# Attention and two expert layers on one core: the first group's next scores issued between a slot's two products, and two tiles one slot later

## The chip, the core and the metric

The kernel runs on one core of a Trainium2 chip. A core has four compute engines, each with an in-order queue of its own: TensorE (PE, with its weight loads as PEld), VectorE (DVE), ScalarE (ACT) and GpSimd (POOL). SyncE (SP) issues most of the DMA transfers. An engine waits for another through semaphores, and what stands behind a waiting instruction in the same queue waits too. The metric is the time of one execution on the device in microseconds (us).

## The reference, cut to what matters

Three stages follow one another: attention over keys and values pooled by 8, a layer with the gate `h * cos(h)`, and a layer of 8 experts of which each token uses one.

```python
# attention: batch 8, heads 8, seq 576, head_dim 64
k_p = k.reshape(B, H, Sp, 8, D).mean(axis=3); v_p = ...   # 72 pooled keys
scores = scale * q @ k_p.T
scores = scores - max(scores);  attn = exp(scores);  attn /= sum(attn) + 1e-9
x = attn @ v_p                       # to 4608 tokens x 512
h = x @ w_in                         # 512 -> 2048
x2 = (h * cos(h)) @ w_out            # 2048 -> 512
expert = argmax(x2 @ w_gate)         # 8 experts
out = gate * relu(x2 @ w1[expert]) @ w2[expert]
```

## The kernel before

The 4608 tokens are worked through in 12 groups of 384 (`g`), each of three tiles of 128 tokens. A group has 16 slots (`s`), one for each 128 columns of the hidden layer. In every slot the order is written out by hand, and each engine's queue keeps it:

- `mm1(s)`, on PE: the first product of the slot, 12 matmuls into one of two banks `HB[s % 2]`. It needs that bank back from `chain_b(s - 2)`.
- `mm2(s - 2)`, on PE: the second product, 9 matmuls on `gh` and `gl` of two slots earlier.
- `chain_a(s)`: ACT scales (L382) and rounds (L383), DVE subtracts (L385), ACT takes the sine (L386).
- `chain_b(s)`: DVE multiplies and frees the bank (L391), ACT rounds to `gh` (L392), POOL makes the rest `gl` (L393). In group 0 the `chain_b(s - 1)` is issued inside slot `s`.
- `ex[s]`: a list of further work, issued at the slot's end.

In group 0 alone the weights are also decoded, by `weights()`, which `chain_a` calls between L383 and L385: `w_bits(s + 3)` puts six DVE operations (two each of L497, L498 and L499) through the two PSUM banks 6 and 7 and has `chain_b(s - 1)` after the second of them; `w_parts(s + 2)` has two ACT casts and two POOL subtractions (L504, L505), `w_scale(s + 4)` two ACT operations (L492), and `w_load(s + 5)` two DMA loads. There are 16 pairs, so `w_bits` ends with slot 12 and `w_parts` with slot 13.

The attention of group 1 is prepared in group 0 by `ex`. For a tile `i`, `scores` has 16 PE matmuls (32 for the tile that lies across two batches) into banks 6 and 7, then on DVE a maximum and a subtraction for each bank (L322, L324), then an exponential on ACT (L330). `norm` has a sum on DVE (L335), which needs the exponential, two small DVE operations and a POOL multiplication (L338). `transp` has eight PE transposes through the same two banks (L345) and a copy on ACT (L349) and on DVE (L351). Tile 1 is kept where the decoded pair 14 has been, and tile 2 where pair 15 has been, so their subtractions wait until POOL has read these pairs. At the end of slot 14 DVE has four sums of the values (`pool_v`, L304) as well; `transp(2)` is issued in slot 15 between the two products, and `pv` (L362 on PE), the attention products of group 1, right behind the 16 slots.

The sine and the exponential are in different function tables of ACT; a table load stands in ACT's queue where the function changes.

Of the kernel before, what the change touches and what calls it, by code (L numbers as in the profile page):

```python
# [14 lines left out]
AF = mybir.ActivationFunctionType  # L15
# [14 lines left out]
NCH = DFF // 128  # L30
# [46 lines left out]
def attention_moe_kernel(ctx, tc, qT, kT, vP, w_in, w_out, wg, w1, w2, cst, tri, wgt, out, dbg=None):  # L77
    nc = tc.nc
    PE, ACT, DVE, POOL, SP = nc.tensor, nc.scalar, nc.vector, nc.gpsimd, nc.sync
# [175 lines left out]
    atts = [pxp.tile([128, H * KP], F32, name="att")] + [w_tmp(6 + i)[:, 0:576] for i in range(2)]  # L255
    atts = [x.rearrange("p (h k) -> p h k", h=H) for x in atts]
# [46 lines left out]
        t = vraw.pop((b, c))  # L303
        DVE.tensor_reduce(vp[b % 2][:, 128 * c:128 * c + 128], t.rearrange("p (f j) -> p f j", j=8), axis=AX.X, op=ALU.add)  # L304

    def scores(T, i, act=False):
        t0 = i * TP
        att, mx, rs = atts[i % len(atts)], mxs[:, i], rss[:, i]
        b0, b1 = T * TP // S, (T * TP + TP - 1) // S
        sc = [rot(), rot()]  # L310
        for pr in range(4):
            for h, r in enumerate((slice(0, 64), slice(64, 128))):
                o = sc[h][:, KP * pr:KP * pr + KP]
                if b0 == b1:
                    PE.matmul(o, lhsT=qs[r, pr, t0:t0 + TP], rhs=kp[b0 % 2][r, pr], start=True, stop=True)
                else:
                    PE.matmul(o[0:64], lhsT=qs[r, pr, t0:t0 + 64], rhs=kp[b0 % 2][r, pr], start=True, stop=True)
                    PE.matmul(o[64:128], lhsT=qs[r, pr, t0 + 64:t0 + TP], rhs=kp[b1 % 2][r, pr], start=True, stop=True)
        vs = [x[:, 0:288].rearrange("p (h k) -> p h k", h=4) for x in sc]
        for hf in range(2):  # L320
            m = mx[:, hf::2]
            DVE.tensor_reduce(m, vs[hf], axis=AX.X, op=ALU.max)  # L322
            if not act:
                DVE.tensor_tensor(att[:, hf::2], vs[hf], m.unsqueeze(2).to_broadcast([128, 4, KP]), op=ALU.subtract)  # L324
        if act:
            DVE.tensor_scalar(mx, mx, -1.0 / 64.0, None, op0=ALU.mult)
            for h in range(H):
                ACT.activation(att[:, h], vs[h % 2][:, h // 2], AF.Exp, scale=1.0 / 64.0, bias=mx[:, h:h + 1], accum_out=rs[:, h:h + 1])
        else:
            ACT.activation(att, att, AF.Exp, scale=1.0 / 64.0)  # L330

    def norm(i, act=False):
        att, rs = atts[i % len(atts)], rss[:, i]
# [34 lines left out]
    def mm1(s):  # L368
        o = HB[s % 2][:, 0:GT]
        n = 0  # L370
        for c in range(4):
            wh, wl = WI[:, 0, c, s * 128:s * 128 + 128], WI[:, 1, c, s * 128:s * 128 + 128]
            for a, x in ((wh, xTh), (wh, xTl), (wl, xTh)):
                PE.matmul(o, lhsT=a, rhs=x[:, c], start=n == 0, stop=n == 11)  # L374
                n += 1
# [198 lines left out]
    norm(0, True)  # L574
    pool_v(0, 1)
    scores(2, 2)
    norm(1, True)
    norm(2)
# [38 lines left out]
        return [E1[0][:, 1024 * k:1024 * k + 1024].rearrange("p (c t) -> p c t", c=4)[:, :, 128 * i:128 * i + 128] for k in range(2)]  # L617

    for g in range(NG):
        ex = {s: [] for s in range(NCH)}  # L620

        def at(s, f, *a):
            ex[s].append(lambda: f(*a))

        if g + 1 < NG:
            for i in range(3):
                if g == 0:
                    at((9, 12, 13)[i], scores, 3 * (g + 1) + i, i)
                    at((9, 12, 13)[i], norm, i)
                    if i < 2:  # L630
                        at((11, 14)[i], transp, i)
                else:
                    at(1 + 4 * i, scores, 3 * (g + 1) + i, i)
                    if i == 0 and g > 1:
                        at(1, route_exp, g - 2)
                    at(1 + 4 * i, norm, i)
                    at(4 + 4 * i, transp, i)
            if g + 2 < NG:
                at(10 if g > 0 else 14, load_q, g + 2)
        dots = {}  # L640
        if g > 0:
            last = g == NG - 1
            n = 0
            for s, k in enumerate((0, 4, 4, 4, 4, 4, 4) if last else (0, 1, 3, 3, 2, 1, 3, 2, 2, 1, 2, 4)):
                dots[s] = list(range(n, n + k))
                n += k
            if last:
                at(1, route_exp, g - 2)
                at(7, route_sel, g - 1)
                at(8, route_exp, g - 1)  # L650
                at(9, route_pos)
                for i in range(3):
                    at(10 + i // 2, route_put, i)
            else:
                at(12, route_sel, g - 1)
                at(14, route_pos)
        if g > 1:
            for i in range(3):
                at(2 + i // 2, route_put, i)
        for b in range(1, B):  # L660
            if g == max(0, b * S // GT - 2):
                if b == 1:
                    at(11, lambda: (kvb.__setitem__(slice(0, None), ring[2:4] + ring[0:2]), kvb_i.__setitem__(0, -1)))
                for c in range(4):
                    if b == 1:
                        at(c // 2, pool_k, b, c)
                        at(11 + c // 2, load_v, b, c)
                        at(14, pool_v, b, c)
                    else:
                        at(2 + 2 * c, pool_k, b, c)  # L670
                        at(2 * c, load_k, b, c)
                if b > 1:
                    for c in range(4):
                        at((7, 10, 12, 14)[c], pool_v, b, c)
                        at((5, 7, 10, 12)[c], load_v, b, c)
        for s in range(NCH):
            mm1(s)
            first_x = s == NCH - 1 and g == NG - 1
            if first_x:
                for i in range(2):  # L680
                    tx_pe(i, XP[i])
            if s == 0 and g > 0:
                mm2(15)
            if s == NCH - 1 and g == 0:
                transp(2)
            elif s == NCH - 1 and g + 1 < NG:
                for c in range(2):
                    pv(g + 1, c)
            if s >= 2:
                mm2(s - 2)  # L690

            def weights():
                w_bits(s + 3, {2: lambda: chain_b(s - 1)} if s > 0 else {})
                w_parts(s + 2)
                w_scale(s + 4)
                w_load(s + 5)

            if g == 0:
                chain_a(s, weights)
            elif g == NG - 1 and 6 < s < 15:  # L700
                c = (s - 7,)
                chain_a(s, lambda: split(0, -50, 0, c, False, (0,)))
            else:
                chain_a(s)
            if s == 0 and g > 0:
                evac(g - 1)
            if first_x:
                E1.append(ep.tile([128, 4096], F32R, name="E1", tag="e1"))
                for i in range(2):
                    tx_parts(XP[i], *unit_x(i))  # L710
            todo = dots.get(s, [])
            if todo:
                route_dot(g - 1, todo.pop(0))
            if g > 0 or s == NCH - 1:
                chain_b(s)
            for n in todo:
                route_dot(g - 1, n)
            if s == NCH - 1 and 0 < g < NG - 1:
                pv(g + 1, 2)
                pv(g + 1, 3)  # L720
            for f in ex[s]:
                f()
            if g == NG - 1:
                if s == 0:
                    SP.dma_start(out=EF[:, 0:4096], in_=w1[0])
                    SP.dma_start(out=wgs, in_=wg)
                    blank()
                if s == 7:
                    SP.dma_start(out=wgb, in_=w2[0])
                if s == 9:  # L730
                    DVE.tensor_scalar(run[:, 0:1], run[:, 0:1], float(EARLY * TP), None, op0=ALU.max)
                if s == 11:
                    SP.dma_start(out=first, in_=tbl[0:EARLY * TP].rearrange("(t p) two -> p t two", p=TP))
                if s == 13:
                    POOL.tensor_copy(firsti, first[:, :, 0])
                    gather(0, 0)
                    gather(0, 1)
                if 6 < s < 15:
                    split(0, -50, 0, c, False, (1,))
        if g == 0:  # L740
            SP.dma_start(out=wgb, in_=wgt.unsqueeze(0).to_broadcast([128, NE * DM]))
            kvb[:] = ldt
            del atts[1:]
            pv(1, 0)
            pv(1, 1)
            mm2(14)
            pv(1, 2)
            pv(1, 3)
        elif g < NG - 1:
            mm2(14)  # L750
# [174 lines left out]
    V, W, L, T = {}, {}, {}, {}  # L925
# [106 lines left out]
```

## Time and profile before

| | |
|---|---|
| median of 3 runs | 1498.08 us (1495.77 to 1500.23) |
| the profiled execution, its own time | 1489.18 us |
| its span, first to last instruction | 1487.4 us |
| mean granted TensorE clock | 0.988 |
| busy share of the span: PE, DVE, ACT, POOL | 96%, 61%, 52%, 32% |

The profiled execution is 8.90 us shorter than the median of the runs; between its time and its span lie 1.78 us. A matmul's end is modelled, so busy shares of PE say less than the gaps between its instructions. In a timeline row the bracket gives the idle time of the engine right before the row and what ended it; a row that merges several instructions of one form has its count at the end. The times in a row are pipelined: an instruction's duration can reach a little into the next one's.

### The profile page before, as it was taken

What the parts mean: (1) busy time and instruction counts of PE and PEld (TensorE: products, weight loads), DVE (VectorE), ACT (ScalarE), POOL (GpSimd) and SP (SyncE); (2) the same over time, 40 slices, a digit from 0 to 9 for tenths busy, and PEclk for the clock granted to TensorE, in tenths of its full rate; (3) what the DMA queues carried; (4) which work ended last, traced back from release to release, by engine and by line L of the source; (5) the groups of instructions that cost most, each with busy time, mean ns of one, the idle gap of its engine ahead of it and who ended that gap; (6) DMA issues with size and microseconds to landing.
All of it is one profiled execution on the core that took longest, in us unless ns stands there. A gap on an engine that the chain in (4) does not pass through costs nothing. (4 is left out here: it accounts for less than half of the span.)

```text
span 1487.4 us, 24388 instructions
## 1 busy us (share of the span) xinstructions
PE 1426.9 (96%) x8394; PEld 1250.2 (84%) x8394; DVE 913.4 (61%) x1997; ACT 777.6 (52%) x1431; POOL 480.5 (32%) x450
## 2 busy tenths in 40 slices
PE   5889999999999999999999999999999999899996
PEld 3768888888888888888888888789999998789996
DVE  7987868675868675868776667552432524772221
ACT  5986656565656565657566655731411413661111
POOL 2662323242424232424232334422221413442121
PEclk9999999999999999999999999999999999999998
DMA  9542112000211100212100002218331402511110
GB/s 299 192 154 108 62 38 69 30 23 30 62 45 43 53 5 22 70 38 62 46 22 22 22 1 80 72 38 342 110 142 38 171 29 82 199 38 60 32 50 23
DMA packets 44119, 112.48 MB, mean 76 GB/s; under 512 B 8025, under 2 KB 24033, under 8 KB 41712
## 3 DMA queue, kind: packets, MB, share of 16 engines
q1 hardware_dynamic: 33184, 78.20, 16.2%
q0 software_dynamic: 9840, 18.98, 4.1%
q10 hardware_dynamic: 864, 12.58, 2.2%
q8 instruction: 100, 1.64, 0.5%
q14 instruction: 131, 1.07, 0.3%
HBM read 98.95 MB, written 20.25 MB: 80 GB/s over the span
## 5 line engine op out<-in xcount | busy, mean ns | idle before, releaser
L374 PE MATMUL bank<-xh,WI 128*128 128x384 f32 x1536 | 435.3, 344 | 10.1 <-DVE tA L391 5.9
L400 PE MATMUL bank<-wb,gh 128*128 128x512 f32 x1152 | 395.1, 397 | 0.0
L374 PEld LDWEIGHTS bank<-xh,WI 128*128 128x128 f32 x1536 | 282.2, 189 | 27.7 <-DVE tA L391 12.6
L400 PEld LDWEIGHTS bank<-wb,gh 128*128 128x128 f32 x1152 | 216.6, 188 | 53.4 <-issue 5.3
L374 PE MATMUL bank<-xl,WI 128*128 128x384 f32 x768 | 259.5, 338 | 1.0 <-DVE xl L366 1.0
L400 PE MATMUL bank<-wb,gl 128*128 128x512 f32 x576 | 227.9, 396 | 0.2 <-POOL gl L393 0.2
L432 DVE SCALAR_TENSOR_TENSOR E<-x2t,wgb 128x512 bf16<-128x512 f32 x264 | 217.9, 825 | 2.1
L782 PEld LDWEIGHTS bank<-E,wb 128*128 128x128 f32 x1632 | 210.4, 192 | 8.9 <-DVEq L809 0.6
L782 PE MATMUL bank<-E,wb 128*128 128x256 f32 x1632 | 213.7, 284 | 0.2 <-DVEq L809 0.2
L792 PE MATMUL bank<-wb,xh 128*128 128x512 f32 x816 | 209.5, 395 | 0.0
L785 ACT ACTIVATE xh<-bank 128x256 fp32r<-128x256 f32 x136 | 52.2, 384 | 279.2 <-PE bank L782 273.2
L786 DVE SCALAR_TENSOR_TENSOR xh<-bank,xh 128x256 fp32r<-128x256 f32 x136 | 57.6, 423 | 218.3 <-ACT xh L785 103.8
L393 POOL TENSOR_TENSOR gl<-E,gh 128x384 fp32r<-128x384 f32 x96 | 104.8, 1092 | 268.2 <-ACT gh L392 234.8
L393 POOL TENSOR_TENSOR gl<-tA,gh 128x384 fp32r<-128x384 f32 x96 | 107.2, 1116 | 247.3 <-ACT gh L392 241.3
L792 PEld LDWEIGHTS bank<-wb,xh 128*128 128x128 f32 x816 | 145.7, 189 | 25.2 <-issue 0.2
L374 PEld LDWEIGHTS bank<-xl,WI 128*128 128x128 f32 x768 | 145.2, 189 | 5.9 <-DVE xl L366 1.9
L195 POOL DMA_INDIRECT E<-x2d,E x66 | 71.2, 1079 | 239.0 <-PE bank L609 213.2
L400 PEld LDWEIGHTS bank<-wb,gl 128*128 128x128 f32 x576 | 108.3, 188 | 18.1 <-POOL gl L393 0.5
L385 DVE SCALAR_TENSOR_TENSOR tA<-bank,tA 128x384 f32<-128x384 f32 x96 | 52.2, 544 | 76.1 <-ACT bank L383 75.7
L385 DVE SCALAR_TENSOR_TENSOR E<-bank,E 128x384 f32<-128x384 f32 x96 | 53.2, 554 | 68.5 <-ACT bank L383 68.5
L234 DVE TENSOR_TENSOR wb<-stg,wb 128x512 fp32r<-128x512 f32 x95 | 70.2, 779 | 23.3 <-ACT wb L232 21.6
L386 ACT ACTIVATE E<-E 128x384 f32<-128x384 f32 x96 | 50.4, 525 | 63.3 <-DVE E L385 62.8
(195 smaller groups left out, 1870.8 us busy)
## 6 DMA issues: line engine op xcount, KB each, us to landing
stg<-w SPq DMA_DIRECT2D x8, 2048.0 KB
stg<-w ACTq DMA_DIRECT2D x6, 2048.0 KB
x2d<-x2t SPq DMA_DIRECT2D x36, 256.0 KB
early<-qT SPq DMA_DIRECT2D x11, 768.0 KB
E<-kT SPq DMA_DIRECT2D x24, 288.0 KB
E<-vP SPq DMA_DIRECT2D x24, 288.0 KB
wgb<-w_in SPq DMA_DIRECT2D x13, 512.0 KB
wgb<-w_out SPq DMA_DIRECT2D x13, 512.0 KB
```

Of the source, the lines that this page charges most:

```text
L195: POOL.indirect_dma_start(out=xg[i], out_offset=None, in_=x2d[0:n], in_offset=bass.IndirectOffsetOnAxis(ap=column(u, i)[0], axis=0), bound ...
L234: ins.append((POOL if pool and c in (2, 5) else DVE).tensor_tensor(l, s, h.bitcast(F32), op=ALU.subtract))
L374: PE.matmul(o, lhsT=a, rhs=x[:, c], start=n == 0, stop=n == 11)
L385: DVE.scalar_tensor_tensor(a, r, MAGIC, a, op0=ALU.subtract, op1=ALU.subtract)
L386: ACT.activation(a, a, AF.Sin, scale=-TWOPI)
L393: POOL.tensor_tensor(gl[s % 2], a, gh[s % 2].bitcast(F32), op=ALU.subtract)
L400: PE.matmul(ACC[i], lhsT=a[:, sl], rhs=w_tile(s)[:, DM * w:DM * w + DM], start=s == 0 and n == 0, stop=s == NCH - 1 and n == 2)
L432: DVE.scalar_tensor_tensor(junk, x2[i], 1.0, wgb[:, DM * e:DM * e + DM], op0=ALU.mult, op1=ALU.mult, accum_out=lgs[:, i, e:e + 1])
L782: PE.matmul(o, lhsT=w_tile(4 * w + s // 2)[:, f], rhs=x[:, c], start=n == 0, stop=n == 11)
L785: ACT.activation(h, o, AF.Relu)
L786: DVE.scalar_tensor_tensor(l, o, 0.0, h.bitcast(F32), op0=ALU.max, op1=ALU.subtract)
L792: PE.matmul(OP[i], lhsT=a[s % 3][:, 128 * i:128 * i + 128], rhs=w_piece(w, s), start=s == 0 and n == 0, stop=s == 7 and n == 2)
```

## The change

`scores` no longer issues the exponential in group 0; that goes to a function of its own, `scores_exp`. The matmuls, maxima and subtractions of `scores` are issued from a table `mid`, right after `mm1(s)` and so ahead of `mm2(s - 2)`, `chain_a(s)` and the decoding in it. The exponential and `norm` stay in `ex[s]`, at the slot's end. Tile 0 stays in slot 9; tile 1 goes from slot 12 to 13, tile 2 from 13 to 14. `transp(0)` stays in slot 11, `transp(1)` in slot 14 (now ahead of the exponential of tile 2), `transp(2)` in slot 15. Groups 1 to 10 are as they were.

```diff
-    def scores(T, i, act=False):
+    def scores(T, i, act=False, then=True):
...
-        else:
-            ACT.activation(att, att, AF.Exp, scale=1.0 / 64.0)
+        elif then:
+            scores_exp(i)
+
+    def scores_exp(i):
+        att = atts[i % len(atts)]
+        ACT.activation(att, att, AF.Exp, scale=1.0 / 64.0)
...
-        ex = {s: [] for s in range(NCH)}
+        ex, mid = {s: [] for s in range(NCH)}, {}
...
                 if g == 0:
-                    at((9, 12, 13)[i], scores, 3 * (g + 1) + i, i)
-                    at((9, 12, 13)[i], norm, i)
+                    mid[(9, 13, 14)[i]] = lambda i=i: scores(3 + i, i, then=False)
+                    at((9, 13, 14)[i], scores_exp, i)
+                    at((9, 13, 14)[i], norm, i)
                     if i < 2:
                         at((11, 14)[i], transp, i)
...
             mm1(s)
+            mid.get(s, bool)()
```

## Rows read from the trace of the kernel before

**Rows 1.** Busy time of each engine, instructions, granted clock, by stretch.
```profile
121.00:200.00 79.00, 78.77 (x451) 68.27 (x450) 59.75 (x136) 49.47 (x85) 22.48 (x20) 1.00 0.22 77
```

**Rows 2.** Waits of PE from 78.8 to 127 us: total, times, longest.
```profile
PE bank L315 <- DVE x2t L499: 2.0, 2, 1.8
...
PE bank L317 <- DVE x2t L499: 0.6, 2, 0.5
```

**Rows 3.** Timeline of DVE, slots 9 to 15 of group 0: start, us, what.
```profile
78.79 1.27 DVE L497 TENSOR_SCALAR bank<-wgb 128x512 uint32<-128x512 uint32 x2
...
82.83 0.55 DVE L385 SCALAR_TENSOR_TENSOR E<-bank,E 128x384 f32<-128x384 f32 x1
83.91 0.46 DVE L322 TENSOR_REDUCE mxs<-bank 128x4 f32<-128x288 f32 x1 [0.53 <-PE bank L315]
...
86.46 0.75 DVE L335 TENSOR_REDUCE rss<-att 128x8 f32<-128x576 f32 x1 [0.75 <-ACT att L330]
...
87.58 1.26 DVE L497 TENSOR_SCALAR bank<-wgb 128x512 uint32<-128x512 uint32 x2
...
102.56 0.55 DVE L385 SCALAR_TENSOR_TENSOR tA<-bank,tA 128x384 f32<-128x384 f32 x1
103.37 0.46 DVE L322 TENSOR_REDUCE mxs<-bank 128x4 f32<-128x288 f32 x1 [0.26 <-PE bank L318]
...
104.99 0.46 DVE L324 TENSOR_TENSOR E<-bank,mxs 128x288 f32<-128x288 f32 x1 [0.24 <-POOL wb L505]
106.20 0.75 DVE L335 TENSOR_REDUCE rss<-E 128x8 f32<-128x576 f32 x1 [0.75 <-ACT E L330]
...
108.86 0.46 DVE L322 TENSOR_REDUCE mxs<-bank 128x4 f32<-128x288 f32 x1 [0.57 <-PE bank L315]
110.96 0.46 DVE L324 TENSOR_TENSOR x2t<-bank,mxs 128x288 f32<-128x288 f32 x1 [1.65 <-POOL wb L505]
...
112.22 0.46 DVE L324 TENSOR_TENSOR x2t<-bank,mxs 128x288 f32<-128x288 f32 x1 [0.44 <-POOL wb L505]
113.43 0.75 DVE L335 TENSOR_REDUCE rss<-x2t 128x8 f32<-128x576 f32 x1 [0.75 <-ACT x2t L330]
...
120.53 0.68 DVE L351 COPY early<-bank 72x512 f32<-72x512 f32 x1
```

**Rows 4.** Timeline of PE, slots 9 to 15 of group 0.
```profile
78.30 0.39 PE L400 MATMUL bank<-wb,gh 128*128 128x512 f32 x1
...
97.29 0.42 PE L374 MATMUL bank<-xh,WI 128*128 128x384 f32 x1
...
107.71 1.11 PE L315 MATMUL bank<-E,early 64*128 64x72 f32 x16
...
121.12 1.57 PE L362 MATMUL bank<-early,E 72*64 72x192 f32 x16
```

**Rows 5.** Timeline of ACT, slots 9 to 14 of group 0.
```profile
83.96 1.28 ACT L330 ACT_TABLE_LOAD   x1
85.75 0.69 ACT L330 ACTIVATE att<-att 128x576 f32<-128x576 f32 x1 [0.51 <-DVE att L324]
...
92.05 1.28 ACT L386 ACT_TABLE_LOAD   x1
93.34 0.52 ACT L386 ACTIVATE tA<-tA 128x384 f32<-128x384 f32 x1
...
107.86 0.51 ACT L392 CAST gh<-tA 128x384 fp32r<-128x384 f32 x1 [0.60 <-DVE tA L391]
108.28 1.14 ACT L504 CAST wb<-x2t 128x512 fp32r<-128x512 f32 x2
```

**Rows 6.** Timeline of PE: the longest wait between two products of group 0.
```profile
43.21 0.69 PE L374 MATMUL bank<-xh,WI 128*128 128x384 f32 x1 [4.51 <-DVE tA L391]
```

**Rows 7.** Busy time by stretch around that wait; the granted clock is third from last.
```profile
40.00:45.00 5.00, 1.79 (x6) 1.79 (x7) 5.00 (x10) 4.77 (x9) 2.19 (x3) 0.60 0.60 212
45.00:50.00 5.00, 5.00 (x20) 4.54 (x19) 5.00 (x9) 3.60 (x8) 2.76 (x3) 0.72 0.62 210
```

## The prediction

> **What bounds the kernel now.** I read the windows first, to see where a lost microsecond can be won back. Behind group 0 PE is busy for 78.77 of 79 us at full clock [rows 1], and its share of 96% of the whole span says the same of most of the rest; so whatever group 0 ends earlier or later by is carried to the end undiminished. Then I read PE's waits in slots 9 to 15. Scores wait for the decoding to leave their two banks, 2.0 us for tile 0 and 0.6 us for tile 1 [rows 2]. These are the waits that the new place of the scores can take away. But a wait of PE is only the shadow of whoever is late, so I read DVE's timeline third. In slots 9 to 12 DVE has decoding, two chain operations, and in some slots scores; and the last thing that holds up the attention products of group 1 is a DVE copy at 120.53, behind which they start at 121.12 [rows 3, 4]. From 78.79, where slot 9's decoding starts, to that copy, DVE does a fixed list of work. The change drops none of it and adds none. So the question is one of bookkeeping: **how long does DVE stand idle between 78.79 and that copy, before and after?**
>
> Before, the waits that belong to the scores are nine rows [rows 3]: 0.53 and 0.75 in slot 9; 0.26, 0.24 and 0.75 in slot 12; 0.57, 1.65, 0.44 and 0.75 in slot 13. Together 5.94 us. The waits in slots 10 and 11 belong to work that keeps its place, and I leave them out on both sides.
>
> **The change, part by part.** I walk the queues with durations from these rows. The instructions are the same in number; the function-table loads too, three for the exponential and three back to the sine.
>
> *Tile 0, slot 9, the matmuls.* PE is through its first product at 78.30 [rows 4]. DVE's decoding of slot 8 leaves the second bank at about 78.4, so scores start near 78.45. From the first score matmul to the first maximum pass 1.15 us where nothing is in the way (107.71 to 108.86) [rows 3, 4]; the maximum starts at 79.6. DVE, free at 78.79, is idle for **0.8**. Maxima and subtractions take 1.8 (83.91 to the exponential at 85.75 less the handover) [rows 3, 5], and only then do decoding and `chain_b(8)` follow, 4.04 us (78.79 to 82.83), and L385, 0.55 [rows 3]. This ends at 79.6 + 1.8 + 4.04 + 0.55 = 86.0.
>
> *Tile 0, the exponential.* Here is the point of the whole prediction. Before, ACT did the sine, loaded the exponential's table (83.96, 1.28 us) while DVE was busy with maxima and subtractions, and then still waited 0.51 us for DVE [rows 5]; DVE waited only 0.75 us for the exponential. Now DVE has done maxima and subtractions before, and has nothing left between L385 and the sum L335. The sine waits for L385; the load stands behind the sine, the exponential behind the load. From the end of L385 (83.38, which is 83.91 less the wait of 0.53) to the load passed 0.58, the load takes 1.28, exponential to sum 0.71 (85.75 to 86.46) [rows 3, 5]: DVE is idle for 0.58 + 1.28 + 0.71 = **2.6**. The sum starts at 88.6, and with 1.12 us of normalization (86.46 to 87.58) DVE reaches slot 10's decoding at 89.7 instead of 87.58: 2.1 later. The scores' own wait on PE is gone, but PE now waits ahead of `mm1(10)` and `mm1(11)` for `chain_b`, which stands in DVE's queue behind the scores.
>
> *Slots 10 to 12.* DVE keeps these 2.1 us. The transposes of tile 0 still wait for slot 11's decoding, so `mm1(12)` starts at 97.29 + 2.1 = 99.4 [rows 4]. Slot 12 loses its scores: L385 ends at 102.56 + 0.55 + 2.1 = 105.2 [rows 3].
>
> *Tile 1, slot 13.* PE must first do `mm1(12)`, `mm2(10)`, `mm1(13)`. From 97.29 to 107.71 it did two slots of products and one set of scores [rows 4]; without 0.6 of waits [rows 2] and about 1.05 of scores that is 8.77 for four products, or 6.6 for three. Scores start at 106.0, the maximum at 107.2: DVE is idle for **2.0**. Then 1.8 of maxima and subtractions (no wait for POOL any more: pair 14 is long read), and 0.97 for L391 and L385 (from the sum's 106.20 + 1.12 to 108.86 - 0.57) [rows 3]. ACT meanwhile has after L391: the cast L392 0.42 (107.86 to 108.28), two casts of `w_parts` 1.1, sine with handover 0.58, load 1.28, exponential 0.71 [rows 3, 5], together 4.1; less DVE's 0.48 for L385, DVE is idle for **3.6**.
>
> *Tile 2, slot 14.* PE is early, so the maximum doesn't wait, and pair 15 has been read by POOL by then. But ACT's table is the exponential's, from slot 13. After L391 it does the cast 0.42, the load for the sine 1.28, the sine 0.58, the copy of `transp(1)` about 0.5, the load for the exponential 1.28, the exponential 0.71: 4.8. DVE covers 0.48 of it with L385 and 0.6 with its own copy (0.68 by its row) [rows 3, 5]: idle for **3.7**. Only then come the sum, the `pool_v` sums and the last copy.
>
> *Sum.* After: 0.8 + 2.6 + 2.0 + 3.6 + 3.7 = 12.7. Before: 5.94. The attention products start **6.8 us later**. One thing is late behind them: slot 15's sine must now load its table, which it had before; `chain_b(15)` and the last attention products move a little, and I put 0.3 for it (bounds 0 and the load's 1.28). So **+7.1 us**.
>
> A rule speaks of the loads. In the rows a load starts at 92.05, takes 1.28, and the sine starts at 93.34, right behind it [rows 5]. The Trainium skill, ScalarE: Activation LUTs, "What ACT_TABLE_LOAD costs", gives 1283 ns for the load and some 1380 ns more for a drain, 2.66 us for each switch. The trace agrees with the first figure and shows no drain between a load and the next function; by the page's total the four loads on DVE's way would cost 4 x 1.38 = 5.5 us more and the sum would be +12.6 (an estimate).
>
> *What the other queues do.* The weight loads on SP are issued by the end of a decoding step, and move with DVE; the load of the next queries now waits for the scores of slot 14 instead of 13, and is needed only in group 1's slot 1, over 20 us later. I cost both at nothing; group 1's attention would wait if that cover went.
>
> **The rivals.** *PE's clock falls (later still).* After `mm1(15)`, at about 119.4, PE has nothing until POOL has normalized tile 2: sum at 121.8, 1.12 on DVE, some 1.3 on POOL, so until 124.2, 4.8 us. In group 0 a wait of 4.51 us [rows 6] was followed by a granted clock of 0.60 and then 0.72 over 10 us [rows 7], that is, the 1.2 GHz level from 43.2 to about 47.8, which costs half of 4.6, or 2.3. Here DVE's `pool_v` hides some 0.5 of it. Price +1.8: in all +8.9, 1507.0. Against it: behind the shorter waits of slots 9 to 12 [rows 2] the clock stands at 1.00 from 121 on [rows 1], and the second case rests on one wait.
>
> *The waits are smaller than I walk them.* If ACT is quicker through slots 13 and 14, or PE earlier at the scores, the five idle times shrink. With only slot 9's net 2.1 and half of the rest, (6.8 - 2.1) / 2 = 2.35, it is +4.5, and down to +2: 1500 to 1502.6.
>
> *The other side: the scores' waits on PE are won.* If DVE weren't on the path, PE would gain the 2.0 and 0.6 [rows 2] and lose nothing: -2.6, 1495.5. This holds if DVE's three waits ahead of the sums stay short. They are 2.25 before and 9.9 in my walk; the loss vanishes if they come to 9.9 - 6.8 = 3.1, about 1.0 each, which needs the exponential's table to be in place before the sine is done. ACT's queue order speaks against it.
>
> *Each switch of the table costs a second time its load,* since ACT may have to run empty first where its work is packed closer: four times 1.28 [rows 5], 5.1 more, +12.2, 1510.3. The rows at 92.05 and 93.34 speak against it [rows 5]. It is the mechanism of the Trainium skill's drain, above.
>
> **How the numbers follow.** The sum is made against the profiled execution, 1489.18 us; the median of the runs shown is 8.90 above it, and I add the difference to the median: 1498.1 + 7.1 = **1505.2**. Chances: the forecast, +4.5 to +8, 0.50; the clock falls, +8 to +10, 0.25; smaller waits, +1 to +4.5, 0.13; the gain, 0.07; the drain, 0.05. A change of 0.3% is 4.5 us, about what a measurement of this kernel can tell from none. Faster by more than that needs more than PE's waits can give: 0.04. Within it: the rest of the gain, 0.03, and the smaller waits, 0.13, with a little of the forecast's lower edge: 0.18. Slower: 0.78. The range takes in forecast, clock and the upper half of the smaller waits, and leaves out the gain and the drain: 1500.5 to 1509.5.
>
> **What would show it.** In the changed profile: no wait of score matmuls for L499; L335 in slots 9, 13 and 14 with waits of some 2.6, 3.6 and 3.7 us for L330; table loads right behind the sine; PE waits for L391 ahead of `mm1(10)` and `mm1(11)` and some 4.8 us ahead of `transp(2)`; attention products near 128. I am wrong if the sums' waits stay near 0.75, or if something behind group 0 gives the time back.

## The result, and the profile after

| | before | changed |
|---|---|---|
| median of 7 runs each | 1498.13 us (1495.77 to 1500.82) | 1507.47 us (1504.48 to 1510.18) |
| ratio, 95% interval | | 1.0057 (1.0047 to 1.0068) |
| span of the profiled execution | 1487.4 us | 1505.8 us |
| mean granted TensorE clock | 0.988 | 0.984 |

The change makes the kernel slower by 0.57%, by the ratio about 8.5 us; the two medians lie 9.34 us apart. The forecast was 1505.2 with a range of 1500.5 to 1509.5; the measured median lies in it.

In the changed kernel lines behind `scores` have moved by four and more: the sum L335 is L339, the chain's L385 and L391 are L389 and L395, the exponential L330 is L334, the copies L349 and L351 are L353 and L355. First DVE's timeline, slots 8 to 15 of group 0, the rows that answer to [rows 3]:

```profile
78.29 0.56 DVE L389 SCALAR_TENSOR_TENSOR tA<-bank,tA 128x384 f32<-128x384 f32 x1
79.50 0.46 DVE L322 TENSOR_REDUCE mxs<-bank 128x4 f32<-128x288 f32 x1 [0.66 <-PE bank L315]
...
88.38 0.75 DVE L339 TENSOR_REDUCE rss<-att 128x8 f32<-128x576 f32 x1 [2.57 <-ACT att L334]
...
106.46 0.46 DVE L322 TENSOR_REDUCE mxs<-bank 128x4 f32<-128x288 f32 x1 [1.41 <-PE bank L318]
...
112.92 0.75 DVE L339 TENSOR_REDUCE rss<-E 128x8 f32<-128x576 f32 x1 [3.58 <-ACT E L334]
...
121.28 0.75 DVE L339 TENSOR_REDUCE rss<-x2t 128x8 f32<-128x576 f32 x1 [3.83 <-ACT x2t L334]
...
126.86 0.68 DVE L355 COPY early<-bank 72x512 f32<-72x512 f32 x1
...
130.41 0.56 DVE L395 TENSOR_TENSOR E<-bank,E 128x384 f32<-128x384 f32 x1 [1.95 <-ACT E L390]
```

The five waits of these rows up to the copy take the place of nine. They come to 0.66 + 2.57 + 1.41 + 3.58 + 3.83 = 12.05 us against 5.94 before: 6.1 more, and the copy at the end stands at 126.86 instead of 120.53 [rows 3], 6.33 later. Three of the five are one and the same wait, the sum for the exponential. ACT's timeline in slots 13 to 15 shows why it is so long:

```profile
110.37 0.52 ACT L390 ACTIVATE E<-E 128x384 f32<-128x384 f32 x1
110.91 1.28 ACT L334 ACT_TABLE_LOAD   x1
112.20 0.69 ACT L334 ACTIVATE E<-E 128x576 f32<-128x576 f32 x1
...
116.43 0.52 ACT L396 CAST gh<-E 128x384 fp32r<-128x384 f32 x1 [2.45 <-DVE E L395]
116.97 1.28 ACT L390 ACT_TABLE_LOAD   x1
118.26 0.53 ACT L390 ACTIVATE tA<-tA 128x384 f32<-128x384 f32 x1
...
119.27 1.28 ACT L334 ACT_TABLE_LOAD   x1
120.57 0.68 ACT L334 ACTIVATE x2t<-x2t 128x576 f32<-128x576 f32 x1
...
128.56 1.28 ACT L390 ACT_TABLE_LOAD   x1
```

ACT waits for `chain_b` ahead of its cast L396, and from there to the exponential no bracket stands in its rows: it is working off sine, load, exponential in order (in slot 14 a load ahead of the sine as well), and DVE's queue stands behind the last of them. Compare [rows 5], where the exponential itself waited 0.51 us for DVE: before, the load had run beside DVE's work. PE's timeline, with the rows that answer to [rows 4], shows the shadow of it:

```profile
83.02 0.44 PE L378 MATMUL bank<-xh,WI 128*128 128x384 f32 x1 [1.18 <-DVE tA L395]
91.27 0.69 PE L378 MATMUL bank<-xh,WI 128*128 128x384 f32 x1 [3.77 <-DVE E L395]
...
123.82 1.92 PE L349 MATMUL bank<-consts,x2t 128*72 128x128 f32 x8 [5.02 <-POOL x2t L342]
...
128.52 1.57 PE L366 MATMUL bank<-early,E 72*64 72x192 f32 x16
...
132.60 1.57 PE L366 MATMUL bank<-early,E 72*64 72x192 f32 x16 [0.21 <-DVE xl L370]
```

The waits for the score banks [rows 2] are gone, and in their place PE waits 1.18 and 3.77 us for `chain_b` and 5.02 us for tile 2's normalization. Behind the two long waits the granted clock is lower; the windows (clock third from last):

```profile
91.00:96.00 5.00, 4.73 (x14) 4.63 (x15) 4.41 (x9) 4.72 (x8) 3.52 (x3) 0.50 0.31 107
121.00:126.00 5.00, 2.18 (x10) 1.85 (x11) 4.65 (x7) 1.31 (x3) 1.15 (x1) 0.78 0.00 0
```

The first attention products start 128.52 - 121.12 = 7.40 us later. How far the loss is carried shows in DVE's copy of a result, first behind group 0 and then at the end of group 11, each time before and changed:

```profile
131.06 0.68 DVE L405 COPY x2t<-bank 128x512 f32<-128x512 f32 x1
138.25 0.68 DVE L409 COPY x2t<-bank 128x512 f32<-128x512 f32 x1
...
974.96 0.69 DVE L405 COPY x2t<-bank 128x512 f32<-128x512 f32 x1 [0.49 <-PE bank L400]
982.43 0.69 DVE L409 COPY x2t<-bank 128x512 f32<-128x512 f32 x1 [0.38 <-PE bank L404]
```

The distances are 7.19 and 7.47. Nothing behind group 0 gives anything back. The remaining 11 us between the two spans lie in the expert layers and don't belong to the change, as the second profiles below show.

### The profile page after: what moved, and what is told of

The parts are those of the page before. It is cut to its first block, busy times and chain, and to the rows that moved or that the text cites. A ratio compares the mean times of both kernels' runs of the same rounds, so it can differ in the third digit from the quotient of the medians.

```text
span 1505.8 us, 24393 instructions
## 1 busy us (share of the span) xinstructions
PE 1436.7 (95%) x8394; PEld 1257.4 (84%) x8394; DVE 914.3 (61%) x1997; ACT 777.9 (52%) x1431; POOL 480.6 (32%) x450
## 3 DMA queue, kind: packets, MB, share of 16 engines
q14 instruction: 131, 1.07, 0.2%
## 5 line engine op out<-in xcount | busy, mean ns | idle before, releaser
L389 DVE SCALAR_TENSOR_TENSOR tA<-bank,tA 128x384 f32<-128x384 f32 x96 | 52.3, 545 | 76.2 <-ACT bank L387 74.8
L389 DVE SCALAR_TENSOR_TENSOR E<-bank,E 128x384 f32<-128x384 f32 x96 | 53.2, 554 | 68.3 <-ACT bank L387 67.9
```

Of the source, the lines that this page charges most:

```text
L389: DVE.scalar_tensor_tensor(a, r, MAGIC, a, op0=ALU.subtract, op1=ALU.subtract)
```

## The experiments

Executions begin group 0 up to 0.7 us apart. So for all of them the place of the first and second attention products of group 1 is also given from the start of L385 (L389) of slot 8, which is at 78.33 before. Most kernels have one profile here, and the two of before differ by 0.58 us counted from slot 8. In the second one DVE waits 0.44 us in slot 9 for a scaling of the weights on ACT (L492), which itself waits 1.01 us for their DMA instead of 0.45; so a few tenths in this table say nothing.

| kernel | first, us | second, us | first, from slot 8 | second, from slot 8 |
|---|---|---|---|---|
| before | 121.12 | 125.41 | 42.79 | 47.08 |
| before, second profile | 121.50 | 125.79 | 43.37 | 47.66 |
| changed | 128.52 | 132.60 | 50.23 | 54.31 |
| changed, second profile | 128.35 | 132.48 | 50.17 | 54.30 |
| exponential early | 120.24 | 125.05 | 42.45 | 47.26 |
| no table change | 121.31 | 126.13 | 42.94 | 47.76 |
| tile 0 only | 123.14 | 127.43 | 44.79 | 49.08 |
| later slots only | 123.68 | 129.35 | 45.50 | 51.17 |
| tile 0, sum a slot later | 122.08 | 126.37 | 44.06 | 48.35 |
| PE kept busy | 126.83 | 132.50 | 48.60 | 54.27 |
| no sine in slot 15 | 129.10 | 132.90 | 51.21 | 55.01 |
| both of these | 126.24 | 131.05 | 48.60 | 53.41 |
| exponential early, waits filled | 118.81 | 124.88 | 41.02 | 47.09 |

**The exponential early.**

```diff
-                    mid[(9, 13, 14)[i]] = lambda i=i: scores(3 + i, i, then=False)
-                    at((9, 13, 14)[i], scores_exp, i)
+                    mid[(9, 13, 14)[i]] = lambda i=i: scores(3 + i, i, then=True)
```

> The changed kernel, but the exponential is issued on ACT right behind the tile's subtractions, between the slot's two products, and no longer at the slot's end; matmuls, maxima, subtractions, slots and normalization stay as changed. My theory (the loss is DVE waiting ahead of the sum for a function-table load and an exponential that stand behind the sine) expects the three waits of the sum L335 to fall from 2.57, 3.58 and 3.83 us to nothing, the first attention products of group 1 to start at 121 to 123 us instead of 128.52, and the time to come back to that of before within 0.3%. The rival (the scores' maxima and subtractions ahead of the decoding, and the later slots, are the loss) expects the start of the attention products to stay within 2 us of 128.52 and the time 6 to 9 us above before.

One line's place in ACT's queue, and the whole loss is gone: the ratio to before is 0.9985 (0.9973 to 0.9998), medians 1488.17 against 1490.32 on that occasion. The first products, at 120.24, are even a little earlier than expected. ACT's timeline in slot 9 and DVE's sums:

```profile
79.76 1.28 ACT L334 ACT_TABLE_LOAD   x1
81.05 0.68 ACT L334 ACTIVATE att<-att 128x576 f32<-128x576 f32 x1
81.64 0.56 ACT L386 ACTIVATE E<-bank,consts 128x384 f32<-128x384 f32 x1
```

```profile
85.20 0.74 DVE L339 TENSOR_REDUCE rss<-att 128x8 f32<-128x576 f32 x1
85.97 0.98 DVE L340 TENSOR_SCALAR rss<-rss 128x8 f32<-128x8 f32 x1
...
107.62 0.74 DVE L339 TENSOR_REDUCE rss<-E 128x8 f32<-128x576 f32 x1
...
114.61 0.74 DVE L339 TENSOR_REDUCE rss<-x2t 128x8 f32<-128x576 f32 x1
```

No sum waits. The load runs beside the maxima, and the exponential is done 3.5 us ahead of its sum in slot 9, 1.6 and 2.2 us ahead in slots 13 and 14. The number of loads is unchanged. DVE's idle time hasn't gone to nothing: it now waits 1.38 and 1.39 us for ACT ahead of L389 in slots 13 and 14, and counted as in the prediction it comes to 5.76 us, about the 5.94 before. So the loss is gone, and little is won. The rival falls: scores ahead of the decoding, in the later slots, lose nothing by themselves.

**No table change.**

```diff
-        ACT.activation(att, att, AF.Exp, scale=1.0 / 64.0)
+        ACT.activation(att, att, AF.Identity if g == 0 else AF.Exp, scale=1.0 / 64.0)
...
+    g = -1
```

> The changed kernel, but in group 0's three tiles the exponential is replaced by the identity, which needs no other function table than the sine's; the output is not the reference's in group 1. My theory expects no table loads in slots 9 to 15, the waits ahead of the three sums to fall by one load each in slots 9 and 13 (2.57 to 1.3, 3.58 to 2.3) and by two in slot 14 (3.83 to 1.3), so the attention products to start 5.1 us earlier or a little more, at 122.5 to 123.5 instead of 128.52. The rival, that the place of the scores is the loss and the loads lie beside it, expects 127 or later.

Everything stands where the change put it, but the loads are gone. DVE's sums:

```profile
87.05 0.75 DVE L339 TENSOR_REDUCE rss<-att 128x8 f32<-128x576 f32 x1 [1.17 <-ACT att L334]
...
109.44 0.75 DVE L339 TENSOR_REDUCE rss<-E 128x8 f32<-128x576 f32 x1 [2.15 <-ACT E L334]
...
115.67 0.75 DVE L339 TENSOR_REDUCE rss<-x2t 128x8 f32<-128x576 f32 x1 [1.05 <-ACT x2t L334]
```

The waits fall by 1.40, 1.43 and 2.78, one load, one load and two loads, each a little over 1.28. From slot 8 on the first products come at 42.94 instead of 50.23: 7.3 earlier, also earlier than expected, and more than the 5.6 of the waits. Where PE waited 5.02 us ahead of tile 2's transposes it now waits 2.24, and the granted clock from 121 to 131 us is 1.00 instead of 0.78 and 0.87; the eight transposes take 1.07 us instead of 1.92. So the loads on DVE's way are about all of the loss; the time itself says nothing here, as other values choose other experts.

**Tile 0 only.**

```diff
-                    mid[(9, 13, 14)[i]] = lambda i=i: scores(3 + i, i, then=False)
-                    at((9, 13, 14)[i], scores_exp, i)
-                    at((9, 13, 14)[i], norm, i)
+                    if i == 0:
+                        mid[9] = lambda: scores(3, 0, then=False)
+                        at(9, scores_exp, 0)
+                    else:
+                        at((9, 12, 13)[i], scores, 3 + i, i)
+                    at((9, 12, 13)[i], norm, i)
```

> Of the change only tile 0's part: its scores go between the products of slot 9, its exponential stays at the slot's end; tiles 1 and 2 are as before, in slots 12 and 13. My theory expects a wait of 2.6 us ahead of the sum in slot 9, DVE 1.9 to 2.1 us late from slot 10 on, and the attention products of group 1 at 123.1 to 123.3 instead of 121.12 (before) and 128.52 (changed). The rival, that PE's won wait for the banks (2.0 us) is a gain, expects 119 to 121.

```profile
88.42 0.75 DVE L339 TENSOR_REDUCE rss<-att 128x8 f32<-128x576 f32 x1 [2.57 <-ACT att L334]
```

The products start at 123.14, 2.0 behind before, as worked out. PE has won its 2.0 us ahead of the scores and lost them again, with 1.2 and 3.8 us ahead of `mm1(10)` and `mm1(11)`.

**The later slots only.**

```diff
-                    at((9, 12, 13)[i], scores, 3 * (g + 1) + i, i)
-                    at((9, 12, 13)[i], norm, i)
+                    at((9, 13, 14)[i], scores, 3 * (g + 1) + i, i)
+                    at((9, 13, 14)[i], norm, i)
```

> The kernel before with one difference: tile 1's scores, exponential and normalization go whole from slot 12 to 13, tile 2's from 13 to 14, all at the slots' ends. My theory has this as a part of the loss that is not the exponential's: DVE has nothing to do in the place of the scores in slot 12 and waits for PE in 13 and 14. Worked out queue by queue: the attention products of group 1 at 122.5 to 124.5 (1.5 to 3.5 us later than before). The rival, that the later slots only save DVE's waits for POOL (0.24, 1.65 and 0.44), expects 118.5 to 121.

The edit is made on the kernel before. The first products start at 123.68, inside the theory's bounds and outside the rival's: 2.7 us late from slot 8 on, 4.1 at the second products. In slot 9 this profile is like the second one of before, with a wait of DVE of 0.36 us for L492; against that one it is 2.1 and 3.5 us late. DVE's new waits:

```profile
113.26 0.69 DVE L351 COPY early<-bank 72x512 f32<-72x512 f32 x1 [1.57 <-PE bank L345]
115.34 0.46 DVE L322 TENSOR_REDUCE mxs<-bank 128x4 f32<-128x288 f32 x1 [1.40 <-PE bank L315]
...
127.17 0.56 DVE L391 TENSOR_TENSOR E<-bank,E 128x384 f32<-128x384 f32 x1 [1.95 <-ACT E L386]
```

The waits for POOL are gone as the change meant, but at the slots' ends DVE now waits for PE, and in slot 15 for a sine that has to load its table, since tile 2's exponential stands in slot 14. The later slots cost nothing only with the scores early, as the first experiment has them; the parts don't add up one by one.

**Tile 0, the sum a slot later.** The edit is shown against the kernel of "tile 0 only".

```diff
-                    at((9, 12, 13)[i], norm, i)
+                    at((10, 12, 13)[i], norm, i)
```

> Tile 0's part of the change alone, with its exponential still behind the sine at the end of slot 9, but the sum and the rest of the normalization one slot later, in slot 10; tiles 1 and 2 as before. My theory (what costs is DVE standing in order behind the exponential, not the exponential's lateness itself) expects no wait ahead of the sum and the attention products of group 1 at 121.0 to 122.0, against 123.14 with the sum in slot 9. The rival (the late exponential holds up ACT's following work, and so the chain, wherever the sum stands) expects 123 or later.

The first products start at 122.08, between the two: 0.7 us better than with the sum in slot 9, counted from slot 8, which is hardly more than two profiles of one kernel differ by. The wait of 2.57 is gone, but others have come: tile 2's subtraction waits 2.32 for POOL instead of 1.65 [rows 3], tile 1's 0.72 and 0.43 instead of 0.24, and L340 takes 1.29 us instead of 0.17 (see the end). PE's clock has a part as well: it waited 3.20 us ahead of `transp(0)`, the granted clock from 96 to 101 us is 0.72 (1.00 before), the eight transposes take 1.89 us instead of 1.23, and DVE's copy behind them waits 1.01 us instead of 0.26. DVE's standing in order may be part of the cost, but postponing the normalization puts POOL's share of it behind POOL's other work. This run doesn't decide between the two theories as they were put.

**Both kernels once more.** No edit.

> The changed kernel once more, on another occasion. In the first timing it was 0.57% above before (0.47 to 0.68), in the trace 7.5 us of this had come by the end of group 11, and the expert layers behind it took 11 us longer than in the profile of before. My theory (the whole loss lies in group 0, the rest is the occasion) expects the attention products of group 1 at 128.4 to 128.6 us again, 7.4 to 7.6 us at the end of group 11, expert layers within 3 us of those of before on the same occasion, and a time 7 to 9 us above before. The rival (the change also lengthens the expert layers, by some 10 us) expects a time 15 to 20 us above before.

> The kernel before, for a second profile on the occasion of the changed kernel's. My theory expects group 0 as in the first profile, within 0.3 us, and expert layers like those of the changed kernel within 3 us. The rival expects expert layers some 10 us shorter than the changed kernel's.

The ratio is 1.006 (1.0045 to 1.0074), medians 1497.66 and 1489.8. The spans of the two profiles are 1493.5 and 1485.6, 7.9 apart; 7.3 of it are there at the end of group 11 (982.24 and 974.94), and the rest, the expert layers, takes 511.3 and 510.7 us. In the first profile of the changed kernel it took 1505.8 - 982.43 = 523.4: that belongs to the occasion. The rival falls. Some expectations are missed by a little: the first products come at 128.35 instead of 128.4 to 128.6, those of before 0.38 us later than in its first profile (the wait of 0.44 us in slot 9), and at the end of group 11 it is 7.3 instead of 7.4 to 7.6. The copies behind group 0 lie 6.70 us apart here instead of 7.19.

**PE kept busy, slot 15 without its sine, and both.** Two things might account for what lies between the copy's 6.33 and the 7.19 at the second products: the lower clock behind PE's 5.02 us, or the sine's table load in slot 15.

```diff
             if s == NCH - 1 and g == 0:
+                for _ in range(2):
+                    o = rot()[:, 0:GT]
+                    for n in range(10):
+                        PE.matmul(o, lhsT=WI[:, 0, n % 4, 0:128], rhs=xTh[:, n % 4], start=n == 0, stop=n == 9)
                 transp(2)
```

> The changed kernel with twenty more matmuls of 384 columns (results unused) between the first product of slot 15 and the transposes of tile 2, where PE waited 5.0 us for POOL and the granted clock fell behind. My theory (the lower clock is real, but hidden: the attention products are held up by DVE's late chain anyway) expects a wait of 1.3 to 1.7 us there, the eight transposes in 1.0 to 1.1 us instead of 1.92, the first attention products at 127.0 to 127.4 instead of 128.52, and the second ones still at 132.2 to 132.7, the copy of group 0's first result at 138.0 to 138.4. The rival (the clock sets the end of group 0) expects the second attention products and the copy to come 1 us earlier or more, at 131.5 and 137.2.

```profile
119.21 3.74 PE L694 MATMUL bank<-xh,WI 128*128 128x384 f32 x20 [0.50 <-ACT early L353]
123.73 1.07 PE L349 MATMUL bank<-consts,x2t 128*72 128x128 f32 x8 [0.78 <-POOL x2t L342]
...
126.83 1.57 PE L366 MATMUL bank<-early,E 72*64 72x192 f32 x16
...
132.50 1.57 PE L366 MATMUL bank<-early,E 72*64 72x192 f32 x16 [0.79 <-DVE xl L370]
```

The transposes take 1.07 instead of 1.92, and the granted clock stays at 1.00 from 116 us on. The first products come 1.7 earlier (somewhat earlier than expected), the second ones not at all: 0.58 and 0.79 us of waits for `gl` and for `xl` take up what was won. The copy of the first result stands at 138.16 against 138.25.

```diff
-        ACT.activation(a, a, AF.Sin, scale=-TWOPI)
+        ACT.activation(a, a, AF.Identity if g == 0 and s == 15 else AF.Sin, scale=-TWOPI)
```

> The changed kernel with the sine of slot 15 of group 0 replaced by the identity, so that slot 15 needs no table load; the output is not the reference's for the first three tiles. My theory (this load is what lies between 6.33 us at DVE's last copy and 7.19 us at the second attention products) expects the wait ahead of L395 in slot 15 to fall from 1.95 to some 0.6 us, and the second attention products at 131.4 to 131.9 instead of 132.60. The rival (the lower clock of PE is the difference) expects them to stay at 132.3 to 132.7.

The wait ahead of L395 falls to 0.59 as expected, but the second products stay, at 132.90: against my expectation. In this run the lower clock lasted longer (0.62 and 0.70 in the windows from 121 and 126 on, against 0.78 and 0.87), and PE now set the time. Hence the two edits together:

> Both edits of the last two runs at once on the changed kernel: the twenty extra matmuls that keep PE busy ahead of tile 2's transposes, and the identity in place of the sine of slot 15 in group 0 (wrong there, no table load). Each alone left the second attention products of group 1 where they were (132.50 and 132.90 against 132.60). My theory now: the lower clock and slot 15's table load end at the same place and cover each other, so only both together move it; the second attention products at 131.4 to 131.9, with no wait of PE ahead of them. If they stay at 132.4 or later, a third thing holds them.

```profile
131.05 1.57 PE L366 MATMUL bank<-early,E 72*64 72x192 f32 x16
```

The second products start at 131.05, a little earlier than expected and without a wait, or 53.41 from slot 8 on instead of 54.31. Each thing covers the other, and the two of them hold 0.9 us. What is left is 53.41 - 47.08 = 6.33 us against before, as much as DVE is late at its last copy; so no third thing is needed. This rests on one profile of each kernel.

**A version that fills the waits.** On top of the early exponential:

```diff
-                        at(14, pool_v, b, c)
+                        if c in (0, 3):
+                            at(12 if c == 0 else 14, pool_v, b, c)
...
                 w_bits(s + 3, {2: lambda: chain_b(s - 1)} if s > 0 else {})
+                if s in (13, 14):
+                    pool_v(1, s - 12)
...
-            if s == NCH - 1 and g == 0:
-                transp(2)
-            elif s == NCH - 1 and g + 1 < NG:
+            if s == NCH - 1 and 0 < g < NG - 1:
...
             if s >= 2:
                 mm2(s - 2)
+            if s == NCH - 1 and g == 0:
+                transp(2)
```

> A version meant to beat both: the changed kernel with the exponential right behind the subtractions, and three of the four sums of the values moved from the end of slot 14 into places where DVE waited in that version (end of slot 12: 1.36 us; slot 13 and slot 14 ahead of L385: 1.38 and 1.39), and the transposes of tile 2 behind the second product of slot 15 (PE waited 1.63 ahead of them). If the waits of DVE are filled, the attention products start 0.5 to 1.5 us earlier than in the version without the move (120.24), and the time is 0.10% to 0.30% below before. If PE's own list bounds slots 14 and 15, it stays within 0.3 us of 120.24.

The first products come at 118.81, 1.4 earlier than with the early exponential alone, as the filled waits promised. The time is 0.9984 of before (0.9975 to 0.9993), no better than 0.9985. PE's timeline shows where it went:

```profile
120.36 0.49 PE L404 MATMUL bank<-wb,gh 128*128 128x512 f32 x1
121.44 0.52 PE L404 MATMUL bank<-wb,gl 128*128 128x512 f32 x1 [0.58 <-POOL gl L397]
121.77 1.04 PE L404 MATMUL bank<-wb,gh 128*128 128x512 f32 x2
122.61 0.63 PE L404 MATMUL bank<-wb,gl 128*128 128x512 f32 x1
...
124.88 1.71 PE L366 MATMUL bank<-early,E 72*64 72x192 f32 x16
```

`mm2(14)` runs at the lower clock from 121.77 on (0.63 for a matmul that elsewhere takes 0.40), and by the second products the 1.4 us have shrunk to 0.2. The granted clock is 0.50 from 122 to 125 us, the 1.2 GHz level, although PE's last waits before it fell were of 0.23 and 0.58 us; why it fell here no run shows. Both versions beat the kernel before by about 0.15%, with intervals that come within 0.1% of no gain.

## Why the prediction was right

- **The yardstick, DVE's idle time up to the last copy: right in size, too simple in one point.** 6.1 us more idle time was measured against 6.8, and 6.33 at the copy. But the first attention products need only the first of the two copies of each tile, ACT's; on PE they stand behind `mm2(13)` and tile 2's transposes, which wait for POOL. The second products need DVE's copy. DVE is behind both ways, so the sum holds; the sentence that the copy holds up the first products was wrong. They start at 121.12 before, and the copy runs until 120.53 + 0.68 = 121.21.
- **The exponential behind the sine: right, and shown.** 2.57, 3.58 and 3.83 us were measured where 2.6, 3.6 and 3.7 were forecast. Taking the exponential forward removes the loss; taking the loads away removes it as well.
- **DVE's wait for the scores:** 0.66 against 0.8 in slot 9, and 1.41 against 2.0 in slot 13. These two terms are the 0.7 by which the sum was too large: for the second I took 1.15 us from the first score matmul to the maximum, from tile 2's matmuls; with tile 1's it was 0.77 (105.69 to 106.46).
- **Slot 15's load:** 0.3 was forecast; with the lower clock it holds 0.9 at the second products. That this surplus and the 0.7 by which the sum was too large nearly cancel is luck: 7.1 forecast, 7.19 and 6.70 at the first copy of a result, 7.47 and 7.3 at the end of group 11.
- **The rival of the clock: it came, at two places, and cost next to nothing.** In slots 10 and 11 DVE's waits stay as they were (0.59, 0.26 and 0.25 us against 0.56, 0.26 and 0.25). In slot 15 it shows at the first products (1.92 us for eight transposes), and at the second ones it is hidden by DVE's chain: with the clock kept up they come 0.1 us earlier. Its price of 1.8 was too high, because I hid it only behind `pool_v` and not behind slot 15; without slot 15's load it does cost 132.90 - 131.05 = 1.85 us (1.6 counted from slot 8). The argument that shorter waits leave the clock at 1.00 doesn't hold in every profile either: in the second one of before the granted clock is 0.50 from 86 to 88 us, behind a wait of 2.40 us.
- **The time alone doesn't tell the two apart.** The measured median, 1507.47, is nearly the 1507.0 of the clock's rival, and 8.5 or 9.3 us lie in its bracket of +8 to +10 and not in the forecast's +4.5 to +8. The traces and the run with PE kept busy decide for the mechanism that was forecast; the size in the first timing came out 1.4 to 2.2 us above it.
- **The drain:** every load took 1.28 us; in slot 13 it stood right behind the sine (110.37 + 0.52, then 110.91), and the exponential stood right behind the load (110.91 + 1.28, then 112.20). Without the loads the waits fell by about 1.40 us for each. The second 1.38 us that the Trainium skill (ScalarE: Activation LUTs, "What ACT_TABLE_LOAD costs") gives for a switch don't show here.
- **The other side:** PE did win its 2.6 us ahead of the scores, and paid them back, with more, ahead of `mm1(10)`, `mm1(11)` and `transp(2)`.

What stays open: 7.3 to 7.9 us in the traces are 0.49% to 0.53%, the ratios are 0.57% and 0.60% with intervals that reach down to 0.47% and 0.45%. Whether something more than group 0 adds to it can't be told from these.

## What to carry to other kernels

When an operation is split, ask of each half what ran beside it. Here the half that moved had been the cover for a table load on ACT; the half that stayed then had nothing in front of it but the load, and an in-order engine stood behind it three times. If a step is moved forward, move its consumer in the other engine's queue with it, or leave something for the waiting engine to do in between.

A wait that disappears from the bottleneck's row is no gain until the engine that caused it has less to wait for: count the idle time of that engine, before and after, over a stretch with fixed work.

## What the runs showed that I had not expected

A tiny DVE operation, 128x8 (L340, L336 before), which takes 0.16 or 0.17 us in all 36 places before and after, took 0.98 us with the exponential early and 1.29 us with the sum a slot later. In both it ended with a POOL subtraction that was running beside it: 85.97 + 0.98 = 86.95 against the POOL row here of the early exponential, which ends at 85.63 + 1.30 = 86.93.

```profile
85.63 1.30 POOL L509 TENSOR_TENSOR wb<-E,wb 128x512 fp32r<-128x512 f32 x1
```

With the sum a slot later it was 90.73 + 1.29 = 92.02 against 90.70 + 1.30 = 92.00. The profile counts it as busy. In group 0 of the runs above it happens four more times: 0.32 us in slot 13 of the early exponential, 0.82 without the table change, 0.99 and 0.32 in the version that fills the waits, each ending 0.03 us behind a POOL row; and wherever this operation took its usual time, no POOL row went on past its end. So a small operation on DVE may cost up to 1.1 us more if it is moved beside POOL's work. The Trainium skill (SBUF — State Buffer, "Who interferes with whom") says that a DVE operation in a two-port mode and a GpSimd operation exclude each other for the whole instruction. The ends above agree with it; that L340 runs in such a mode no trace shows.
